# Keys and queries in one row, first weights in runs of 4 KB, another written list for block 0

## The chip, the core and the metric

The kernel runs on one core of a Trainium2 chip. The core has five engines with an instruction queue each: TensorE (PE in the rows; its weight loads are PEld), VectorE (DVE), ScalarE (ACT), GpSimd (POOL) and SyncE (SP), which here only starts DMA transfers. Each engine runs its own instructions strictly in the order in which they were written; engines wait for each other at semaphores. The metric is the device time of one execution in microseconds (us).

## What is computed

Sparse attention over 8 batches, 8 heads, 576 positions and head size 64, then a feed-forward layer of 4608 tokens with inner size 2048, in float32:

```python
scores = np.matmul(q, k.transpose(0, 1, 3, 2)) / np.sqrt(D)
mask_local = (rel >= 0) & (rel < 32)              # heads 0 to 3
mask_strided = (rel >= 0) & (col % 32 == row % 32) # heads 4 to 7
attn = softmax(where(mask, scores, -1e9))
x = (attn @ v).transpose(0, 2, 1, 3).reshape(B * S, H * D)   # 4608 x 512
h = x @ w_in                                       # 512 x 2048, kept as float64
out = (h / (1 + exp(-h))) @ w_out                  # 2048 x 512, kept as float64
```

## The kernel before

**Attention.** A batch is cut into six groups (`GROUPS`): three of local heads (12 tiles of 32 queries), three of strided heads (8, 8 and 6 tiles). Group number c counts on over the batches: 0 to 5 are batch 0, 6 to 13 belong to the next ones. A group needs its keys and queries (`load_qk`, line 384, into the tile `k`) and its values (`load_v`, into `v`).

**Feed-forward.** Tokens are taken in nine blocks of 512. Matrix products run with each operand split into a high and a low part, three matmuls for one product. The weights come as 64-bit numbers in 32 pieces of 512 KB (`load_piece`, line 343): piece 0 is columns 0 to 127 of `w_in`, after that `w_in` and `w_out` take turns. Block 0 is computed while the weights arrive; each piece is rounded and split on ACT and DVE, and stays in the core.

**The written list.** From the first instruction to the last product but one of block 0, the order of the work is a list of words, `PLAN` (line 145), that `Steps.follow` (line 204) carries out word by word. So the list fixes the order on every engine. The words, with c a group, n a piece and f a chunk of 128 inner columns (0 to 15):

- Attention: `kc` and `vc` loads; `Sc` scores on PE (line 485); `Mc` mask and row minimum on DVE (L513); `Ec` exp on ACT (L531, 6 or 8 steps); `Rc` reciprocal (DVE, L546 and L547); `Nc` scaling (L550); `Tc` transpose on PE and `Pc` its copy out (L560); `Vc` transpose on DVE (L578, L583, groups from 6 on); `Oc` times values (PE, L617, L622 or L637); `Qc`, `Xc` turn a local result back; `Bc` copy of the result into x (L649, L677, L693).
- Weights: `pn` load; `an` two ACT passes (L312, L317); `jn` join (DVE, L323); `bn` high part (L368); `dn` low part (DVE, L372).
- Block operands: `Hbc` and `Lbc`, high (L710) and low part (L714) of columns c of x for block b. `H00` to `L03` belong to block 0, `H10` to `L13` to block 1.
- Chunks of block 0: `hf` and `if`, the two halves of the inner product (PE, L722, 6 matmuls each); `tf` tanh (ACT, L732); `gf` gate (DVE, L754); `wf` and `lf`, high and low part of the gated chunk (L762, L766); `of` the output product (PE, L781, 12 matmuls). Chunk f uses piece 2f-1 of `w_in` (piece 0 for f = 0) and piece 2f+2 of `w_out` (piece 31 for f = 15).
- `~m` is m filler matmuls of 128 columns (PE, L889). `.A`, `.D`, `.P` choose ACT, DVE or POOL where a step may run on several.

The list ends with `o14`. Behind it a planner with fixed costs orders the rest (blocks 1 to 8); the first work there is the inner product of chunk 0 of block 1 on PE, 12 matmuls (L722), then the last output product of block 0.

**Loads.** SP starts nearly all transfers. In batch 0 a group's keys and queries are two transfers (lines 390 and 392; the queries of the first three groups start from ACT); later one transfer of two runs per partition, both as long as the longer of the two (line 388). A piece of `w_in` comes as four runs of 1 KB per partition (line 355), a piece of `w_out` as one run of 4 KB (line 360); the first six pieces in two halves.

Of the kernel before, what the change touches and what calls it, by code (L numbers as in the profile page):

```python
# [107 lines left out]
class Group:  # L108
    def __init__(self, local, first, count):
        self.local, self.first, self.count = local, first, count  # L110
        self.rows = STRIDE if local else KW
# [8 lines left out]

        self.at = [(t % self.n, t // self.n) for t in range(count)]
# [25 lines left out]
M4 E4 Q0 k6 C1 v3 v4 T1 P1.D R2 S3 M3 E3 X0 B0.D a1 T2 P2.D O1 p0 C2 Q1 R4 N4.P S5 M5 k7 O2 X1  # L147
Q2 B1.A R3 N3.D ~2 j1 T4 P4.A E5 H00.D p3 p4 k8 X2 B2.A T3 P3.D a0 L00.P H01.A O4 p5 p2 O3 S6
b1.D B4 R5 N5.D d1 j0 b0.A L01.P T5 P5.D d0 p6 B3 H02.D L02 ~4 O5 B5 H03.D L03 a3 M6 j3
b3.D E6 h0 h1 p7 R6 v7 d3 i0 t0 g0 S8 M8 k10 a5 j5 i1 S7 M7 a2 j2 p9 b5.A d5 w0.D t1 g1  # L150
b2.A d2 h2 p11
S10 l0 i2 a6 j6 v6 h3 a7 j7 o0 a4 i3 b6.D w1.D b7.A p8 j4 d7 t2 g2 h4 b4.A d4 l1 o1 k12 p13 a11
# [6 lines left out]
b21.A d21 b25.A d25 p27 t10 g10 t9 g9 h11 S11 k13 h12 i11 i12 Y0 E9 V7 M11 a24 j24 b24.D d24
p26 w10.A w9.A l9 o9 a27 j27 b27.A l10 t11 g11 t12 S12 g12 d27 M12 E11 R11 N11 a26 j26 O7 B7 v9  # L160
R9 N9 b26.A d26 o10 w11.A l11 w12.A l12 O10 V9 V11 B10 E12 R12 p29 a29 j29 p28 a28 j28 h13 h14
i13 t13 g13 i14 t14 g14 b28.A d28 N12 b29.A d29 O9 V12 v11 B9 o11 w13.A o12 w14.A l14 l13 O11
# [54 lines left out]
def sparse_attention_ffn(ctx: ExitStack, tc: tile.TileContext, kqt, vt, w_in, w_out, out):  # L217
# [165 lines left out]

    def load_qk(a):
        to, of = kbds[kbd_of(a.b, a.at)], kqt[a.b, a.gi]
        if a.b:
            n = max(a.g.nq, a.g.nk)
            load(out=to[:, :, :n], in_=of[:, :, :n])
            return
        load(out=to[:, 0, : a.g.nk], in_=of[:, 0, : a.g.nk])  # L390
        way = nc.scalar.dma_start if a.at < 3 else load
        way(out=to[:, 1, : a.g.nq], in_=of[:, 1, : a.g.nq])

    def load_v(a):
# [418 lines left out]
    def attention_steps(c, due, last=None):  # L813
# [6 lines left out]
        cols = 2 * max(a.g.nq, a.g.nk) if a.b else a.g.nq + a.g.nk  # L820
        k = add(f"k{c}", {"SP": P * cols * 4 / RATE}, t0 - 6, [], lambda: load_qk(a),
                writes=[k_place])
# [1630 lines left out]
```

## Time and profile before

| | us |
|---|---|
| Runs | 807.27, 812.03, 813.08 (median 812.03) |
| Span of the profiled execution | 808.0 |
| PE busy in it | 797.0 (99%) |
| DVE busy | 602.9 (75%) |
| ACT busy | 583.3 (72%) |
| POOL busy | 112.2 (14%) |
| Share of PE in the chain that ended last | 93% |

The profile shows one execution. Its views: the time line of an engine (start, length, engine, line, operation, result<-inputs, count, and in brackets the idle time before it with what ended it); the table of stretches (busy time of each engine and the granted TensorE clock); the transfers by line with their size and the time from start to landing. Successive instructions overlap a little, so the time that a row takes of its engine is best read as the distance to the next row's start.

### The profile page before, as it was taken

What the parts mean: (1) busy time and instruction counts of PE and PEld (TensorE: products, weight loads), DVE (VectorE), ACT (ScalarE), POOL (GpSimd) and SP (SyncE); (2) the same over time, 40 slices, a digit from 0 to 9 for tenths busy, and PEclk for the clock granted to TensorE, in tenths of its full rate; (3) what the DMA queues carried; (4) which work ended last, traced back from release to release, by engine and by line L of the source; (5) the groups of instructions that cost most, each with busy time, mean ns of one, the idle gap of its engine ahead of it and who ended that gap; (6) DMA issues with size and microseconds to landing.
All of it is one profiled execution on the core that took longest, in us unless ns stands there. A gap on an engine that the chain in (4) does not pass through costs nothing.

```text
span 808.0 us, 18904 instructions
## 1 busy us (share of the span) xinstructions
PE 797.0 (99%) x6661; PEld 659.7 (82%) x6661; DVE 602.9 (75%) x1660; ACT 583.3 (72%) x1559; POOL 112.2 (14%) x160
## 2 busy tenths in 40 slices
PE   8999999999999999999999999999999999999998
PEld 5688778888888898888888888888888888888887
DVE  6999896757868898955789999644699945557753
ACT  7999886557688988898895997788846534445451
POOL 6300004667000000015203000000230000000000
PEclk9999999999999999999999999999999999999999
DMA  8987455588999868698887976896567696666676
GB/s 265 316 258 233 133 189 167 208 271 281 310 288 333 263 220 276 225 319 288 296 269 218 277 249 195 242 280 193 181 195 216 197 269 194 194 194 194 194 215 155
DMA packets 150909, 191.13 MB, mean 237 GB/s; under 512 B 38240, under 2 KB 91104, under 8 KB 150816
## 3 DMA queue, kind: packets, MB, share of 16 engines
q1 hardware_dynamic: 149296, 189.21, 74.8%
q8 instruction: 53, 0.87, 0.4%
q10 hardware_dynamic: 1520, 0.72, 0.3%
q14 instruction: 40, 0.33, 0.1%
HBM read 151.09 MB, written 38.80 MB: 235 GB/s over the span
## 4 chain that ended last, share of the span: by engine, by line
PE 93%; DMA 3%; DVE 2%; ACT 1%; issue 1%; SPq 0%; POOL 0%; POOLq 0%; DVEq 0%
PE ps L1586 33%; PE po L2188 19%; PE po L781 16%; PE ps L722 10%; PE ps L2188 6%; PE ps L637 2%; DMA k<-kqt 2%; PE ps L485 1%; PE po L2331 1%; PE po L637 1%; PE ps L476 1%; PE ps L889 1%; DMA v<-vt 1%; DVE stage L2168 1%; ACT stage L2164 0%
## 5 line engine op out<-in xcount | busy, mean ns | idle before, releaser
L1586 PE MATMUL ps<-xop,w 128*128 128x512 f32 (+1 forms) x720 | 143.7, 348 | 0.0
L1586 PE MATMUL ps<-w,w 128*128 128x512 f32 x576 | 138.6, 390 | 0.0
L1586 PEld LDWEIGHTS ps<-xop,w 128*128 128x128 f32 x720 | 118.2, 189 | 18.5
L1586 PEld LDWEIGHTS ps<-w,w 128*128 128x128 f32 x576 | 107.9, 188 | 22.5
L531 ACT ACTIVATE sm<-sm,sums 128x54 f32<-128x54 f32 (+2 forms) x320 | 109.4, 345 | 7.8 <-DVE sums L513 7.7
L2188 PE MATMUL po<-stage,w 128*128 128x512 f32 x456 | 107.0, 390 | 0.0
L2188 PEld LDWEIGHTS po<-stage,w 128*128 128x128 f32 x456 | 85.3, 188 | 17.8
L722 PE MATMUL ps<-xop,w 128*128 128x512 f32 x384 | 94.9, 394 | 0.0
L722 PEld LDWEIGHTS ps<-xop,w 128*128 128x128 f32 x384 | 71.0, 188 | 15.2
L531 ACT ACTIVATION_READ_ACCUMULATOR sm<-sm,sums 128x1 f32 x320 | 60.6, 189 | 0.0
L781 PE MATMUL po<-w,ghi 128*128 128x512 f32 x168 | 52.1, 391 | 0.0
L2168 DVE TENSOR_TENSOR stage<-w,stage 128x512 fp32r<-128x512 f32 x56 | 40.9, 733 | 13.0 <-ACT stage L2164 12.5
L2164 ACT CAST stage<-w 128x512 fp32r<-128x512 f32 x56 | 34.8, 621 | 20.0 <-DVE stage L2168 8.1
L2026 DVE TENSOR_TENSOR w<-ps,w 128x512 f32<-128x512 f32 x44 | 30.0, 686 | 25.2 <-PE ps L1586 24.6
L2064 ACT ACTIVATE w<-w 128x512 f32<-128x512 f32 x45 | 27.6, 629 | 18.6 <-DVE w L2026 18.4
L766 DVE TENSOR_TENSOR glo<-th,ghi 128x512 fp32r<-128x512 f32 x48 | 34.7, 727 | 7.1 <-ACT ghi L762 6.9
L2188 PE MATMUL ps<-stage,w 128*128 128x512 f32 x168 | 39.4, 391 | 0.0
L503 POOL MEMSET sm<- 128x80 f32 (+1 forms) x18 | 2.9, 161 | 247.9 <-ACT pt L604 74.8
L2188 PEld LDWEIGHTS ps<-stage,w 128*128 128x128 f32 x168 | 31.4, 188 | 6.6
L2022 ACT COPY w<-ps 128x512 f32<-128x512 f32 x48 | 27.9, 584 | 12.0 <-PE ps L1586 10.7
L732 ACT ACTIVATE th<-ps 128x512 f32<-128x512 f32 x32 | 18.8, 592 | 24.5 <-PE ps L722 23.5
L604 ACT COPY pt<-sm 32x192 f32<-32x192 f32 (+1 forms) x96 | 34.8, 362 | 1.8
(330 smaller groups left out, 1639.7 us busy)
## 6 DMA issues: line engine op xcount, KB each, us to landing
w<-sums SPq DMA_DIRECT2D x208, 256.0 KB, 3.2
w<-osums SPq DMA_DIRECT2D x160, 256.0 KB, 2.9
sums<-xop SPq DMA_DIRECT2D x16, 512.0 KB, 3.8
osums<-stage SPq DMA_DIRECT2D x16, 512.0 KB, 5.5
v<-vt SPq DMA_DIRECT2D x21, 384.0 KB, 5.2
stage<-w_out SPq DMA_DIRECT2D x14, 512.0 KB, 4.3
k<-kqt SPq DMA_DIRECT2D x14, 477.0 KB, 5.6
stage<-w_in SPq DMA_DIRECT2D x12, 512.0 KB, 4.1
```

The lines of the kernel that those rows point to most:

```text
L531: nc.scalar.activation(out=self.s_sb[:, c, h], in_=self.s_sb[:, c, h], func=AF.Exp, bias=self.peaks[:, c, h : h + 1], scale=-1.0, accum_ou ...
L604: copy[by](out=self.pt[to, odd], in_=of)
L722: nc.tensor.matmul(ph, weight(0, wi, fc)[:, cc // 2, cc % 2 * P : (cc % 2 + 1) * P], x[xi][cc], start=(cc, n) == (0, 0), stop=(cc, n) == ( ...
L766: either[engine].tensor_sub(out=g[1][:, cols], in0=th[:, cols], in1=g[0][:, cols].bitcast(F32))
L781: nc.tensor.matmul(po[tt], g[gi][:, cols], weight(1, wi, fc), start=first and n == 0, stop=last and n == 2,)
L1586: nc.tensor.matmul(bank[:, : right.shape[-1]], left(wi, kt), right[:, kt, xi], start=first and (kt, n) == (0, 0), stop=(kt, n) == (1, 2), ...
L2022: copy_ps(out=unit(place), in_=of())
L2026: nc.vector.tensor_add(out=to, in0=of(), in1=to)
L2064: nc.scalar.activation(out=unit(out), in_=source(), func=AF.Silu)
L2164: copy_ps(out=gated_ops(to.slot)[0], in_=unit(place))
L2168: nc.vector.tensor_sub(out=lo, in0=unit(place), in1=hi.bitcast(F32))
L2188: nc.tensor.matmul(bank(name, key, m), left[:, wi, m * P : (m + 1) * P], right[xi], start=first and (j, i) == (0, 0), stop=(j, i) == (FH - ...
```

## The change

Three things are changed. The arithmetic stays.

1. Keys and queries of a group lie behind each other in one row per partition. In batch 0 they come in two transfers that are the two halves of the row; later in one transfer of one run. The padding to the longer of the two goes: 477 KB become 459.5 KB, 448 become 416, 416 become 400, 359 become 346.5.
2. `w_in` is laid out on the host so that a piece is one run of 4 KB per partition, as `w_out` was.
3. `PLAN` is another list of the same steps. Some steps change engine (B1, H01, b0, b4, b5, b12, b13, b29, w13, H11 to DVE; P5, H03, b6, b8, b23, b24, b30, b31, w1 to ACT). The fillers grow from 24 units to 44.

```diff
@@ load_piece
-        if layer == 0:
-            to = stage.rearrange("p (c f) t -> p c (f t)", c=NP)
-            of = w_in[:, cols].bitcast(I32).rearrange("(c p) f -> p c f", p=P)
-            for some in halved(NP, 2 if i < AHEAD else 1):
-                load(out=to[:, some], in_=of[:, some])
-        else: ...
+        to = stage.rearrange("p f t -> p (f t)")
+        of = (w_out if layer else w_in)[cols, :].bitcast(I32)
+        for some in halved(2 * DM, 2 if i < AHEAD else 1):
+            load(out=to[:, some], in_=of[:, some])
@@ load_qk
-        if a.b:
-            n = max(a.g.nq, a.g.nk)
-            load(out=to[:, :, :n], in_=of[:, :, :n])
-            return
-        load(out=to[:, 0, : a.g.nk], in_=of[:, 0, : a.g.nk])
-        way = nc.scalar.dma_start if a.at < 3 else load
-        way(out=to[:, 1, : a.g.nq], in_=of[:, 1, : a.g.nq])
+        for some in halved(a.g.cols, 1 if a.b else 2):
+            way = nc.scalar.dma_start if some.start and a.at < 3 and not a.b else load
+            way(out=to[:, some], in_=of[:, some])
@@ PLAN, its first line and its last two
-k0 k1 k2 v0 ~7 S0 v1 M0 k4 E0 k3 v2 C0 ~1 S1 k5 M1 E1 ~3 S2 M2 p1 E2 v5 T0 P0.D R1 ~7 S4 O0 R0
-B11 H10.A L10 H11.A h15 S13 M13 L11 p30 a30 j30 b30.D d30 i15 t15 g15 p31 a31 j31 b31.D d31
-H12.A H13.A L12 L13 o13 w15.A l15 o14 E13 R13 N13 V13
+k0 ~7 S0 k1 v0 ~5 S1 M0 M1 k2 E0 E1 ~8 T0 S2 R0 C0 v1 k4 v2 P0.D M2 C1 O0 k3 k5 R1 T1 Q0 E2 P1.D
+H11.D o12 l13.D R13 N13.D h15 H12.A g14 w14.A j30 H13.A b30.A l14.D L13.D o13 d30.D a31 j31 i15
+t15 b31.A g15 w15.A d31.D l15.D E12 V13 L11.D R12 o14 L12.D N12.D V12 L10.D
```

The new list moves work at three places that matter below. The first is ACT in the first quarter of block 0. Before, behind the exps of groups 0, 1, 2, 4 and 3 (34 steps together) stand a1, B1, P4, then E5 (6 steps), B2, a0:

```order
L531 ACTIVATE sm,sums<-sm,sums 128x64 x34
L312 ACTIVATE stage_303<-stage_303 128x512
L317 ACTIVATE stage_303<-stage_303 128x512
L693 COPY xb<-po 128x3x4x32
L560 COPY pt<-po 128x512
L531 ACTIVATE sm,sums<-sm,sums 128x64 x6
L693 COPY xb<-po 128x3x4x32
L312 ACTIVATE stage_485<-stage_485 128x512
L317 ACTIVATE stage_485<-stage_485 128x512
L710 CAST xop<-xb 128x512
L677 COPY xb<-po 128x8x18
L677 COPY xb<-po 128x15x18
```

After, E5 joins the first exps (40 steps), then P4, a0, B2, a1, P5 (line numbers are lower by 7 or 8, but for L312 and L317, which are L315 and L320):

```order
L524 ACTIVATE sm,sums<-sm,sums 128x64 x40
L553 COPY pt<-po 128x512
L315 ACTIVATE stage_492<-stage_492 128x512
L320 ACTIVATE stage_492<-stage_492 128x512
L686 COPY xb<-po 128x3x4x32
L315 ACTIVATE stage_499<-stage_499 128x512
L320 ACTIVATE stage_499<-stage_499 128x512
L553 COPY pt<-po 128x384
L670 COPY xb<-po 128x8x18
L670 COPY xb<-po 128x15x18
L670 COPY xb<-po 128x24x18
L670 COPY xb<-po 128x17x18
```

So E5 has moved ahead of a1 and P4, B1 has left ACT and P5 has come to it; B4 and B3 follow directly.

The second is the end of the list on DVE. Before, it ends with L12, L13 (two rows each), l15, R13, N13 and V13; the row behind is the gate of block 1:

```order
L714 TENSOR_TENSOR xop<-xb,xop 128x64
L714 TENSOR_TENSOR xop<-xb,xop 128x448
L714 TENSOR_TENSOR xop<-xb,xop 128x64
L714 TENSOR_TENSOR xop<-xb,xop 128x448
L766 TENSOR_TENSOR glo<-th,ghi 128x512
L546 TENSOR_SCALAR sums<-sums 128x8
L547 RECIPROCAL sums<-sums 128x8
L550 TENSOR_TENSOR sm<-sm,sums 128x8x54
L578 STREAM_TRANSPOSE pt<-sm 128x256 x2
L583 STREAM_TRANSPOSE pt<-sm 32x256 x4
```

After, V13 (its four small transposes are the first row here), L11, R12, L12, N12, V12 and, as the very last step, L10:

```order
L576 STREAM_TRANSPOSE pt<-sm 32x256 x4
L707 TENSOR_TENSOR xop<-xb,xop 128x64
L707 TENSOR_TENSOR xop<-xb,xop 128x448
L539 TENSOR_SCALAR sums<-sums 128x6
L540 RECIPROCAL sums<-sums 128x6
L707 TENSOR_TENSOR xop<-xb,xop 128x64
L707 TENSOR_TENSOR xop<-xb,xop 128x448
L543 TENSOR_TENSOR sm<-sm,sums 128x576
L571 STREAM_TRANSPOSE pt<-sm 128x192 x2
L576 STREAM_TRANSPOSE pt<-sm 32x192 x4
L707 TENSOR_TENSOR xop<-xb,xop 128x64
L707 TENSOR_TENSOR xop<-xb,xop 128x448
```

So L10, the low part of the first columns of x for block 1, has moved from before M13 to the end of all listed DVE work. On PE the second matmul behind o14, the (high weight, low x) product of chunk 0 of block 1, waits for it.

The third is PE around S13 (`ps<-k`, 16 rows in one). Before, i15 follows it and then o13:

```order
L722 MATMUL ps<-xop,w_8_667 128x512
L485 MATMUL ps<-k_82 64x54 x16
L722 MATMUL ps<-xop,w_8_665 128x512 x2
L722 MATMUL ps<-xop,w_8_667 128x512
L722 MATMUL ps<-xop,w_8_665 128x512 x2
L722 MATMUL ps<-xop,w_8_667 128x512
L781 MATMUL po<-stage_1654,ghi 128x512
```

After, S13 follows i14, and o12, h15, o13, i15 and o14 are still to come:

```order
L715 MATMUL ps<-xop,w_8_693 128x512
L478 MATMUL ps<-k_82 64x54 x16
L774 MATMUL po<-stage_1643,ghi 128x512
L774 MATMUL po<-stage_1646,ghi 128x512
L774 MATMUL po<-stage_1643,glo 128x512
```

So S13 has moved ahead by one output product (o12) and one half (h15). M13 on DVE, which S13 releases, is still the step from which the DVE tail above starts: behind M13 come g13, w13, H11, l13, R13, N13, g14, j30, l14, L13, d30, j31, g15, d31, l15 and then the rows shown.

## Rows read from the trace of the kernel before

**Rows 1.** Table of stretches: stretch, its length, busy us of each engine (instructions), granted clock.
```profile
36.00:60.00 24.00, 23.78 (x193) 19.56 (x194) 23.69 (x61) 23.80 (x62) 0.00 (x0) 1.00 0.81 254
```

**Rows 2.** Time line of PE: start, length, engine, line, result<-inputs, count, idle before.
```profile
24.65 0.91 PE L622 MATMUL po<-pt,v 64*64 64x54 f32 x24 [0.25 <-ACT xb L677]
25.49 4.38 PE L722 MATMUL ps<-xop,w 128*128 128x512 f32 x18
...
36.22 0.82 PE L485 MATMUL ps<-k 64*32 64x64 f32 x48 [1.21 <-DMA k<-kqt]
...
39.87 0.62 PE L781 MATMUL po<-w,ghi 128*128 128x512 f32 x2
```

**Rows 3.** Time line of ACT, the part before PE begins the feed-forward.
```profile
17.31 0.66 ACT L312 ACTIVATE stage<-stage 128x512 f32<-128x512 f32 x1
...
18.43 0.45 ACT L693 COPY xb<-po 128x384 f32<-128x384 f32 x1
...
19.46 0.35 ACT L531 ACTIVATE sm<-sm,sums 128x64 f32<-128x64 f32 x1
...
23.06 0.60 ACT L710 CAST xop<-xb 128x512 fp32r<-128x512 f32 x1
```

**Rows 4.** Time line of DVE in the same part, up to the first x operands.
```profile
17.75 0.62 DVE L661 TENSOR_TENSOR xq<-po,sums 128x192 f32<-128x192 f32 x2
...
20.87 1.11 DVE L368 CAST w<-stage 128x512 fp32r<-128x512 f32 x1
...
24.94 0.83 DVE L372 TENSOR_TENSOR w<-stage,w 128x512 fp32r<-128x512 f32 x1 [0.39 <-ACT w L368]
25.78 0.43 DVE L710 CAST xop<-xb 128x512 fp32r<-128x512 f32 x1
```

**Rows 5.** Transfers of the first 60 us: count, size, median us from start to landing.
```profile
stage<-w_out SPq DMA_DIRECT2D x6, 512.0 KB, 5.1
stage<-w_in SPq DMA_DIRECT2D x6, 512.0 KB, 4.9
```

**Rows 6.** Time line of PE from S13 to block 1's first product.
```profile
115.64 0.69 PE L485 MATMUL ps<-k 64*64 64x54 f32 x32
...
117.75 0.62 PE L781 MATMUL po<-stage,ghi 128*128 128x512 f32 x2
...
123.21 2.88 PE L722 MATMUL ps<-xop,w 128*128 128x512 f32 x12
```

**Rows 7.** Time line of DVE from 112 us on: V11, then M13 to V13.
```profile
112.45 0.63 DVE L578 STREAM_TRANSPOSE pt<-sm 128x192 f32<-128x192 f32 x2
113.11 1.52 DVE L583 STREAM_TRANSPOSE pt<-sm 32x192 f32<-32x192 f32 x4
...
116.55 0.21 DVE L513 CUSTOM_DVE_ANT_0 sm<-ps,mask_strided 128x54 f32<-128x54 f32 x1
...
117.61 0.76 DVE L714 TENSOR_TENSOR xop<-xb,xop 128x64 fp32r<-128x64 f32 x2
...
119.01 0.43 DVE L368 CAST stage<-stage 128x512 fp32r<-128x512 f32 x1
...
123.81 0.69 DVE L766 TENSOR_TENSOR glo<-th,ghi 128x512 fp32r<-128x512 f32 x1
...
124.85 0.61 DVE L550 TENSOR_TENSOR sm<-sm,sums 128x432 f32<-128x432 f32 x1
...
128.11 0.69 DVE L754 SCALAR_TENSOR_TENSOR th<-th,ps 128x512 f32<-128x512 f32 x1
```

**Rows 8.** Time line of PE: the first two fillers of seven units.
```profile
1.36 3.36 PE L889 MATMUL ps<-ident 128*128 128x512 f32 x4 [1.36 <-POOL ident masks.py:199]
...
8.86 1.67 PE L889 MATMUL ps<-ident 128*128 128x512 f32 x4
```

**Rows 9.** Table of stretches, columns as in rows 1: the end of the program.
```profile
804.00:806.00 2.00, 0.32 (x3) 0.12 (x1) 0.45 (x1) 0.00 (x0) 0.00 (x0) 1.00 0.57 95
...
807.30:808.00 0.70, 0.00 (x0) 0.00 (x0) 0.00 (x0) 0.00 (x0) 0.00 (x0) 0.50 0.00 0
```

More of the change, by code (lines that the diff above doesn't have):

```diff
@@ L119, in __init__ @@
         self.nk = self.k0[-1] + KW
+        self.kq = [("k", 0, self.nk), ("q", 0, self.nq)]
+        self.cols = self.nk + self.nq
+        self.q0 = [self.nk + q for q in self.q0]
         self.at = [(t % self.n, t // self.n) for t in range(count)]
@@ L145 @@
 PLAN = """
-k0 k1 k2 v0 ~7 S0 v1 M0 k4 E0 k3 v2 C0 ~1 S1 k5 M1 E1 ~3 S2 M2 p1 E2 v5 T0 P0.D R1 ~7 S4 O0 R0
[L147 to L152, printed above, removed]
@@ L159 @@
[L159 to L162, printed above, removed]
-B11 H10.A L10 H11.A h15 S13 M13 L11 p30 a30 j30 b30.D d30 i15 t15 g15 p31 a31 j31 b31.D d31
-H12.A H13.A L12 L13 o13 w15.A l15 o14 E13 R13 N13 V13
+k0 ~7 S0 k1 v0 ~5 S1 M0 M1 k2 E0 E1 ~8 T0 S2 R0 C0 v1 k4 v2 P0.D M2 C1 O0 k3 k5 R1 T1 Q0 E2 P1.D
@@ new lines @@
+S4 X0 M4 E4 R2 B0.D O1 C2 S3 T2 Q1 ~4 X1 M3 S5 k6 v4 p0 P2.D R4 p1 M5 ~6 O2 E3 v3 N4.P v5 p3 ~6
+T4 S6 B1.D R3 Q2 N3.D M6 E5 P4.A R5 ~3 T3 a0 X2 P3.D H00.D O4 N5.D B2.A p5 ~5 T5 k7 j0 L00.P a1
+P5.A H01.D B4 O3 p4 B3 b0.D j1 d0.D b1.D L01.P O5 B5 h0 H02.D p2 d1.D L02.D H03.A L03.D p7 a3 a5
+j3 h1 b3.D p6 j5 i0 E6 b5.D i1 d3.D t0 d5.D p9 t1 h2 g0 g1 S7 a4 R6 a2 h3 i2 a7 w0.D i3 j4 l0.D
+j2 b2.A j7 d2.D a6 b7.A b4.D t3 o0 d4.D d7.D p11 w1.A g3 l1.D h4 a9 j6 j9 M7 a11 o1 k8 b9.A S8
+d9.D b6.A p10 w3.A t2 a10 p8 k10 d6.D p13 j11 p15 b11.A g2 p12 i4 N6.D v6 j10 w2.A h5 d11.D l2.D
@@ new lines @@
+w10.A d18.D j25 d24.D l10.D S11 i11 p26 b25.A t11 E9 h12 d25.D b20.A M11 o8 w9.A p27 h13 g11 S12
+a26 V7 d20.D M12 i13 i12 a27 l9.D j26 O7 R9 b26.A j27 d26.D B7 b27.A v9 p28 t12 o9 k13 E11 O10
+N9.D w11.A B10 o10 d27.D V9 l11.D p29 R11 O9 v11 o11 a28 B9 g12 w12.A a29 N11.D V11 j28 b28.A
+h14 j29 d28.D O11 l12.D b29.D i14 d29.D B11 S13 M13 t13 t14 H10.A p30 E13 g13 p31 w13.D a30
+H11.D o12 l13.D R13 N13.D h15 H12.A g14 w14.A j30 H13.A b30.A l14.D L13.D o13 d30.D a31 j31 i15
+t15 b31.A g15 w15.A d31.D l15.D E12 V13 L11.D R12 o14 L12.D N12.D V12 L10.D
@@ L241, in sparse_attention_ffn @@
     vbds = [vbd[:, i] for vbd in vbds for i in range(2)]
-    kbds = [const.tile([P, 2, QW], F32, name=f"k{i}") for i in range(KFIRST)]
+    kbds = [const.tile([P, 2 * QW], F32, name=f"k{i}") for i in range(KFIRST)]
     ident = const.tile([P, P], F32, name="ident")
@@ L486, in scores @@
                         self.pss[h][rows, c * self.seen : (c + 1) * self.seen],
-                        kbd[at, 1, g.q0[t] : g.q0[t] + g.rows],
-                        kbd[at, 0, g.k0[t] : g.k0[t] + self.seen], start=True, stop=True,
+                        kbd[at, g.q0[t] : g.q0[t] + g.rows],
+                        kbd[at, g.k0[t] : g.k0[t] + self.seen], start=True, stop=True,
                     )
@@ L819, in attention_steps @@
         k_place, v_place = f"k{kbd_of(a.b, a.at)}", f"v{vbd_of(a.b, a.at)}"
[L820 to L821 removed]
+        k = add(f"k{c}", {"SP": P * a.g.cols * 4 / RATE}, t0 - 6, [], lambda: load_qk(a),
                 writes=[k_place])
@@ L1945, in gated_ops @@
         if OWN_GOPS not in gated_halves and i >= OWN_GOPS:
-            ks = [const.tile([P, 2, T], F32R, name=f"k{n}") for n in range(2)]
-            more = [k[:, half] for k in ks for half in range(2)]
+            ks = [const.tile([P, 2 * T], F32R, name=f"k{n}") for n in range(2)]
+            more = [k[:, half * T : (half + 1) * T] for k in ks for half in range(2)]
             v = const.tile([P, VT * D * 2], F32R, name="v0")
@@ L2385 @@
     none = NP * S
-    q_from = np.full((NG, QW), none)
+    q_from = np.full((NG, 2 * QW), none)
     k_from = np.full((NG, QW), none)
@@ L2431 @@
     turned = np.arange(DM).reshape(4, 4, 32).transpose(1, 0, 2).reshape(-1)
-    kq = np.ascontiguousarray(np.stack([columns(k, k_from), columns(q, q_from)], axis=3))
+    kq = np.zeros((B, NG, P, 2 * QW), q.dtype)
+    of = {"k": columns(k, k_from), "q": columns(q, q_from)}
+    for gi, g in enumerate(GROUPS):
+        at = 0
+        for name, first, n in g.kq:
+            start = first + (g.nk if name == "q" else 0)
+            kq[:, gi, :, at : at + n] = of[name][:, gi, :, start : start + n]
+            at += n
+    w_in = moe_w_in.reshape(NP, P, NFC, P)
     arrays = {
@@ L2437 @@
         "vt": rows(v, v_from),
-        "w_in": np.ascontiguousarray(moe_w_in).view(np.int64),
+        "w_in": np.ascontiguousarray(w_in.transpose(2, 1, 0, 3)).reshape(DFF, DM).view(np.int64),
         "w_out": np.ascontiguousarray(moe_w_out[:, turned]).view(np.int64),
```

21 lines of the change are left out of this document (8 added, 13 removed).

## The prediction

> **What bounds the kernel now.** I read the table of stretches first, then the time lines of PE, ACT and DVE in block 0, then the transfers. From 36 us on PE is busy almost without a gap, but in block 0 it isn't alone: in the stretch from 36 to 60 us PE has 23.78 of 24.00 us, DVE 23.69 and ACT 23.80 [rows 1]. So an earlier product on PE is worth what it saves only where DVE and ACT have its operands ready. Before 36 us PE waits for others. The first half product, h0, starts at 25.49, right behind O5; the scores of group 7 still wait 1.21 us for keys; and the first output product, o0, starts at 39.87 [rows 2]. At the other end of the list all fits: M13 follows S13, and PE starts block 1's first product at 123.21 without a wait [rows 6], while DVE works on its list until 128.11 [rows 7]. The change touches these two ends: what the front gains, the tail can take back.
>
> **The loads.** A piece of `w_in` in runs of 1 KB lands 4.9 us after its start, a piece of `w_out` of the same size in runs of 4 KB after 5.1 us [rows 5]. So longer runs buy no landing time that shows, and I cost them at 0. Keys and queries shrink by 4 to 7 per cent (477 to 459.5 KB). The one load of keys that PE waits for in the front is that of group 7, 1.21 us [rows 2]; in the new order S7 comes later than its keys by the queue's order, so this wait goes with the front's gain below and isn't counted twice. Bounds for all loads together: no loss, at most 0.5 us of gain further on. I take 0.
>
> **The front: PE's lead.** On ACT, before, a1, B1, P4, E5, B2 and a0 take 17.31 to 23.06, 5.75 us; E5 starts at 19.46 in the midst of them [rows 3]. After, E5 follows the earlier exps, so it starts 2.15 us earlier, at 17.31. Up to P5, for which O5 waits, ACT has P4, a0, B2 and a1 (the 5.75 without B1's 0.55) and P5, a copy of about 0.5 (B1, of the same size, has 0.45): 17.31 + 5.20 + 0.5 = 23.0. O5 takes 0.84 (24.65 to 25.49) [rows 2], so h0 can start at 23.9, 1.6 us earlier.
>
> DVE comes too late for all of that. Before, from Q2 at 17.75 to the end of d0 at 25.78 it has 8.03 us, with 0.39 of waiting in it [rows 4]. In the new list the same stretch lacks b1 (1.03, 20.87 to 21.90, slow beside POOL's work), d1 (0.6) and P5 (0.5), and holds M6 (0.8, six of the eight steps of M13's 1.06 [rows 7]) and the casts B1, H01 and b0 (0.47, 0.33 and 0.33, estimates between 0.33 and the 0.46 of the cast at 119.01 [rows 7]): 8.03 - 0.39 - 2.13 + 1.93 = 7.44, so d0 ends at 25.2, or at 25.9 where b0 has b1's trouble with POOL. The third matmul of h0 waits for it. From there I add 0.6 for each of DVE's full-width steps and 0.35 to 0.46 for a cast: L03 ends 2.6 us later, d3 2.5 us after that, g1 1.8 us after that, d2 3.7 us after that, at 35.8 to 36.5. PE meanwhile does h0, h1, i0, i1, h2, S7, h3, i2 and i3, each half product 1.36 (12 matmuls take 2.73, 24 of them 117.75 to 123.21 [rows 6]), and waits for d0, for d1 and, before the second half of S7, for g0, some 1.5 us together. o0 then starts at 36.5 to 37.2 instead of 39.87, with the same work done (i3 in place of S8 and S10). The lead is 2.7 to 3.4; I take 3.0. The bounds: 0, if ACT and DVE lose it again before 110 us; 4.5, if DVE is never late.
>
> **The tail: what L10 costs.** Before, S13 starts at 115.64, M13 0.91 later at 116.55, and PE reaches the second matmul of block 1 at 123.21 + 0.23 = 123.44 [rows 6, 7]. After, S13 stands one output product and one half earlier, 1.5 x 2.73 = 4.09 us, and all is earlier by the lead of 3.0: S13 starts at 108.55, M13 at 109.46. Behind M13 DVE has the listed steps up to L10, and PE's second matmul of block 1 waits for L10. What these steps take: before, M13 to the end of V13 is 116.55 to 128.11, 11.56 us. The new stretch has all of it but two casts b (0.46 each, 119.01 to 119.47), and besides g13, g14 and l14 (0.6 each, a little under the 0.69 of l15's row, since rows overlap), l13 and R12 (1.04 together, as l15 and R13 from 123.81 to 124.85), w13 (0.46), H11 (0.5, two casts), N12 (0.6), V12 (2.2, as V11 from 112.45 to the end of its last row) and L10 (0.67, 117.61 to 118.28) [rows 7]. That is 11.56 - 0.92 + 7.27 = 17.9 us. L10 ends at 109.46 + 17.9 = 127.4, PE's matmul follows at 127.5: **4.0 us later** than before. In general the loss is 7.0 minus the lead. On PE stand only S13 and four times 2.73 behind S13's start, so PE is through with o14 at about 120.2 and then idle for some 7 us. This is the new stall: work of DVE (V13, V12, L11, L12) that nobody waits for at once now stands in front of the step for which PE waits.
>
> **The clock.** The first fillers of seven units took 3.36 us, the same seven units at 8.86 took 1.67 [rows 8]: PE starts on the lower of its two levels, 1.2 GHz, and reaches 2.4 GHz. At the end of the program PE's last work is done at 804.3, the granted clock is 1.00 until 806 and 0.50 from 807.3 on [rows 9]. So an idle time of 7 us can drop the clock, and the restart of block 1 then loses what the program's start loses, 3.36 - 1.67 = **1.7 us**. Bounds: 0 (the clock stays) and 3.4 (twice as long on the lower level). The Trainium skill, TensorE: Matmul & The Clock Gate, Part 1, says that an idle TensorE is throttled to half its clock and gets it back only after sustained activity. The end of this trace agrees for the fall, its start for the return; in the midst of the program no idle time is long enough to show it.
>
> **Sum.** 4.0 + 1.7 + 0 = 5.7 us slower. Behind the list the order of the instructions is the same as before, and PE has hardly a wait that such a shift could fill. On the profiled execution's 808.0 that is 813.7. The three runs and this execution (807.27, 812.03, 813.08, 808.0) have a mean of 810.1, 1.9 below the runs' median of 812.03; I put the sum on this mean: **815.8**.
>
> **Rivals.**
> - *PE doesn't wait for L10, the lead stays.* It decides at 11 us: if DVE's steps from M13 to L10 took no more than PE's work from S13 to o14 (0.6 + 4 x 2.73 = 11.5, less the 0.91 to M13), the kernel would be 3.0 us faster, 807.1. Against it: 17.9 from rows, and the order on DVE is strict.
> - *The lead is lost* (DVE as late as before at every step, or pieces landing late, since p0 and p1 come sooner behind the keys): 7.0 + 1.7 = 8.7 slower, 818.8. For it: DVE, ACT and PE are all near full from 36 to 60 us [rows 1]; against it: the sums of the front.
> - *The clock stays at 2.4 GHz*, or drops late: 4.0 slower, 814.1.
> - *The loads do what the words say and more*: keys that land earlier in later blocks and a front that gains 4.5 leave 810 to 811, no change.
>
> **How the numbers follow.** Forecast (lead 2 to 4, lower clock at the restart) 0.58; lead lost 0.16; clock stays 0.14; no change 0.07; lead kept 0.05. Forecast alone: 814 to 818. The range reaches down to 809, past the 811 of no change but without the lead kept, and up to 822, the lost lead with twice the clock's loss. One per cent (8.1 us) is about what a measurement here can tell from no change: slower by more needs the lost lead with the clock's full loss or runs that scatter upwards, 0.13; faster by more is out of reach of all cases but for scatter, 0.02; within it 0.85.
>
> **What would show it.** In the profile after: h0 near 24 to 25 us and o0 near 37; S13 near 108.5, M13 right behind; DVE without a gap from M13 to L10 for about 18 us; on PE a wait of about 7 us before block 1's first product, ended by DVE L707; the granted clock 0.50 for some us behind it. The prediction is wrong if that wait is under 3 us, if o0 is not earlier than 39, or if PE's later blocks show new waits.

## The result, and the profile after

| | before | after |
|---|---|---|
| Median of the runs (us) | 811.0 (4 runs) | 820.83 (4 runs: 820.41 to 823.85) |
| Ratio, 95% interval | 1 | 1.0144 (1.0109 to 1.0179) |
| Span of the profiled execution | 808.0 | 818.6 |
| o0 starts | 39.87 | 40.81 |
| S13 starts | 115.64 | 113.38 |
| PE's second matmul of block 1 | 123.44 | 133.16 |

By the ratio the changed kernel is 1.44 per cent slower, 11.7 us. The quotient of the two medians would be 1.0121: the four runs before scatter from 807.27 to 813.08, and in the later comparisons, with 17 to 29 runs of it, the kernel before has medians of 809.01 to 809.25. In the changed kernel's profile PE waits once for long, where the prediction said, but the lead that the front was to bring is not there.

The end of the list, PE's time line of the changed kernel (columns as in [rows 2]; it answers to [rows 6]):

```profile
113.38 0.69 PE L478 MATMUL ps<-k 64*64 64x54 f32 x32
...
125.03 0.39 PE L715 MATMUL ps<-xop,w 128*128 128x512 f32 x1
133.16 5.06 PE L715 MATMUL ps<-xop,w 128*128 128x512 f32 x11 [7.74 <-DVE xop L707]
138.02 0.69 PE L774 MATMUL po<-stage,ghi 128*128 128x512 f32 x2
```

Behind S13 PE has work for 11.65 us, then block 1's first matmul, and then 7.74 us of nothing until L10 is done. DVE in the same stretch (answers to [rows 7]):

```profile
114.12 0.21 DVE L506 CUSTOM_DVE_ANT_0 sm<-ps,mask_strided 128x54 f32<-128x54 f32 x1 [1.48 <-PE ps L478]
...
122.02 0.69 DVE L326 SCALAR_TENSOR_TENSOR stage<-stage 128x512 int32<-128x512 int32 x1 [0.35 <-ACT stage L320]
123.14 0.69 DVE L747 SCALAR_TENSOR_TENSOR th<-th,ps 128x512 f32<-128x512 f32 x1 [0.43 <-ACT th L725]
...
125.92 1.79 DVE L576 STREAM_TRANSPOSE pt<-sm 32x256 f32<-32x256 f32 x4
127.74 0.76 DVE L707 TENSOR_TENSOR xop<-xb,xop 128x64 fp32r<-128x64 f32 x2
...
132.34 0.76 DVE L707 TENSOR_TENSOR xop<-xb,xop 128x64 fp32r<-128x64 f32 x2
```

M13 waits for S13, and from its start at 114.12 to the end of L10 (132.34 + 0.76 = 133.10) DVE needs 18.98 us, 0.78 of it waits for ACT. The table of stretches around the wait (columns as in [rows 1]) has the clock:

```profile
126.00:130.00 4.00, 0.00 (x0) 0.00 (x0) 3.90 (x11) 0.65 (x4) 0.00 (x0) 0.74 0.00 0
130.00:133.00 3.00, 0.00 (x0) 0.00 (x0) 2.88 (x9) 0.00 (x0) 0.00 (x0) 0.50 0.00 0
133.00:138.00 5.00, 4.84 (x11) 3.80 (x12) 0.10 (x1) 0.00 (x0) 0.00 (x0) 0.50 0.00 0
```

With PE idle the granted clock falls from 1.00 to 0.50 (from 2.4 GHz to the lower level, 1.2 GHz), and the eleven matmuls behind the wait take 138.02 - 133.16 = 4.86 us, 0.44 each in place of 0.227.

The front, PE's time line of the changed kernel (answers to [rows 2]; L881 are fillers, L549 the transposes T4 and T5, L478 x48 the scores S6):

```profile
18.74 1.56 PE L881 MATMUL ps<-ident 128*128 128x512 f32 x4
20.14 0.60 PE L549 MATMUL po<-ident,sm 128*128 128x128 f32 x4
20.67 0.72 PE L478 MATMUL ps<-k 64*32 64x64 f32 x48
...
24.00 1.35 PE L881 MATMUL ps<-ident 128*128 128x512 f32 x4
25.18 0.49 PE L549 MATMUL po<-ident,sm 128*128 128x128 f32 x3
...
27.37 0.73 PE L715 MATMUL ps<-xop,w 128*128 128x512 f32 x2
28.96 6.95 PE L715 MATMUL ps<-xop,w 128*128 128x512 f32 x28 [0.85 <-DVE w L369]
...
40.81 0.61 PE L774 MATMUL po<-w,ghi 128*128 128x512 f32 x2
```

h0 starts at 27.37, not at 25.49 as before nor at the predicted 23.9, and its third matmul waits for d0. DVE there (answers to [rows 4]; L326 are the joins j0 and j1):

```profile
21.52 0.23 DVE L506 CUSTOM_DVE_ANT_0 sm<-ps,mask 128x64 f32<-128x64 f32 x1 [1.31 <-PE ps L478]
...
23.65 0.55 DVE L543 TENSOR_TENSOR sm<-sm,sums 128x384 f32<-128x384 f32 x1
24.12 1.76 DVE L326 SCALAR_TENSOR_TENSOR stage<-stage 128x512 int32<-128x512 int32 x1
...
26.47 1.76 DVE L326 SCALAR_TENSOR_TENSOR stage<-stage 128x512 int32<-128x512 int32 x1
28.16 0.74 DVE L369 TENSOR_TENSOR w<-stage,w 128x512 fp32r<-128x512 f32 x1
```

And POOL, with N4 and the low parts L00 and L01:

```profile
17.39 1.05 POOL L543 TENSOR_TENSOR sm<-sm,sums 128x512 f32<-128x512 f32 x1 [3.76 <-ACT sm L524]
23.81 1.52 POOL L707 TENSOR_TENSOR xop<-xb,xop 128x512 fp32r<-128x512 f32 x1 [5.37 <-DVE xop L703]
26.30 1.39 POOL L707 TENSOR_TENSOR xop<-xb,xop 128x512 fp32r<-128x512 f32 x1 [0.96 <-DVE xop L703]
```

Two things are to be seen. T4 needs N4, which ends at 18.44; PE is in six units of fillers until 20.14. The scores behind T4 come late, and M6 on DVE waits 1.31 us for them. T5 is held up in the same way: N5 ends at 24.20, T5 starts at 25.18. Second, each join takes 1.76 us where it took 0.69 (the row below, kernel before), beside an operation of POOL, and ends 0.55 us behind that operation's end (25.88 and 25.33; 28.23 and 27.69).

```profile
19.33 0.69 DVE L323 SCALAR_TENSOR_TENSOR stage<-stage 128x512 int32<-128x512 int32 x1
```

Two suspects, then, for the lost lead: the fillers and POOL. The tail and the clock have one each, L10 and the idle time.

Not all of the loss lies ahead of o0. From o0 to S13 PE is busy all the time in both kernels and takes 75.77 us before and 72.57 after, 3.20 less and not the 4.09 that the prediction counts for S13's new place. So 0.9 us of the lead goes there without a wait, and it does so in every run with the new list (72.56 or 72.57 in each). The record doesn't show why.

### The profile page after: what moved, and what is told of

Its sections match the earlier page's. It is cut to its first block, busy times and chain, and to the rows that moved or that the text cites. A ratio compares the mean times of both kernels' runs of the same rounds, so it can differ in the third digit from the quotient of the medians.

```text
span 818.6 us, 18929 instructions
## 1 busy us (share of the span) xinstructions
PE 803.7 (98%) x6673; PEld 663.1 (81%) x6673; DVE 604.3 (74%) x1662; ACT 583.4 (71%) x1557; POOL 114.1 (14%) x160
## 4 chain that ended last, share of the span: by engine, by line
PE 92%; DVE 4%; ACT 3%; SPq 1%; issue 0%; DMA 0%; POOL 0%; POOLq 0%; ACTq 0%
PE ps L1578 33%; PE po L2180 19%; PE po L774 16%; PE ps L715 11%; PE ps L2180 5%; PE ps L630 2%; PE ps L478 1%; PE po L2323 1%; PE po L630 1%; PE ps L469 1%; PE ps L881 1%; ACT sm L524 1%; ACT pt L597 1%; DVE stage L2160 1%; SPq L396 1%
## 5 line engine op out<-in xcount | busy, mean ns | idle before, releaser
L1578 PEld LDWEIGHTS ps<-w,w 128*128 128x128 f32 x576 | 107.9, 188 | 22.5
L715 PE MATMUL ps<-xop,w 128*128 128x512 f32 x384 | 97.4, 402 | 8.6 <-DVE xop L707 7.7
L2018 DVE TENSOR_TENSOR w<-ps,w 128x512 f32<-128x512 f32 x44 | 30.0, 685 | 25.2 <-PE ps L1578 24.6
L725 ACT ACTIVATE th<-ps 128x512 f32<-128x512 f32 x32 | 19.2, 601 | 37.2 <-PE ps L715 34.5
L747 DVE SCALAR_TENSOR_TENSOR th<-th,ps 128x512 f32<-128x512 f32 x32 | 21.8, 683 | 26.0 <-ACT th L725 25.9
## 6 DMA issues: line engine op xcount, KB each, us to landing
k<-kqt SPq DMA_DIRECT2D x14, 459.5 KB, 5.0
```

The source lines that it names most:

```text
L715: nc.tensor.matmul(ph, weight(0, wi, fc)[:, cc // 2, cc % 2 * P : (cc % 2 + 1) * P], x[xi][cc], start=(cc, n) == (0, 0), stop=(cc, n) == ( ...
L1578: nc.tensor.matmul(bank[:, : right.shape[-1]], left(wi, kt), right[:, kt, xi], start=first and (kt, n) == (0, 0), stop=(kt, n) == (1, 2), ...
L2018: nc.vector.tensor_add(out=to, in0=of(), in1=to)
```

## The experiments

Each time stands against the kernel before, run in the same comparison on the same chip, and the ratio is that of the comparison. The runs e1 to e4, e5 to e7 and e8 to e10 are three comparisons on three chips. A difference between two runs is that of their medians; by the ratios it comes out up to half a microsecond larger or smaller.

### Loads or list: e2_loads and e3_list

The change has parts that can be taken one by one: e2_loads is the changed kernel with the list of before, e3_list the kernel before with the new list.

```diff
@@ e2_loads, against the changed kernel
-k0 ~7 S0 k1 v0 ~5 S1 M0 M1 k2 E0 E1 ~8 T0 S2 R0 C0 v1 k4 v2 P0.D M2 C1 O0 k3 k5 R1 T1 Q0 E2 P1.D
+k0 k1 k2 v0 ~7 S0 v1 M0 k4 E0 k3 v2 C0 ~1 S1 k5 M1 E1 ~3 S2 M2 p1 E2 v5 T0 P0.D R1 ~7 S4 O0 R0
...
@@ e3_list, against the kernel before: the same lines the other way round
```

> Parts 1 and 2 of the change alone: keys and queries in one row and w_in in runs of 4 KB, with the list of the kernel before. Theory (the loads are hidden): within 0.2 per cent of the kernel before, 809.5 to 812.5 us, o0 again near 39.9 us. Rival (the loads help the later blocks, where the changed kernel lost some 3 us less in its stalls from 230 to 280 us): 807 to 809 us. Rival (pieces or keys come later and cost the front): 813 us or more, and o0 behind 40.5 us.

Measured: 807.99 us, ratio 0.9985 (0.9971 to 0.9998).

> Part 3 alone: the new list with the transfers of the kernel before. Theory (the list makes the whole difference): 819.5 to 822.5 us, with h0 near 27.4, o0 near 40.8 and the wait for L10 of 7 to 8 us. Rival (the new loads cost the front 1 to 3 us): 817 to 819 us, with o0 at 38 to 40 us.

Measured: 821.30 us, ratio 1.0144 (1.0127 to 1.0162), the ratio of the whole change.

So the list is the whole loss. The loads alone gain 0.15 per cent, 1.2 us, with an interval that just clears 1; the prediction took 0 with at most 0.5. In the trace of e2_loads S7 no longer waits for its keys (before 1.21 us [rows 2]), and o0 starts at 39.26, 0.6 earlier. The gain is within the 0.2 per cent of the theory, but its rival, that the loads help the later blocks, is true as well: at the last product e2_loads is 1.5 us ahead (801.21 against 802.73). The kernel before waits there 0.16 and 0.22 us for transfers near 240 us, and 0.71 us near 257 us without a named releaser; e2_loads has none of the three. The landing times speak for no difference by the length of the runs: w_in pieces of 512 KB land after 5.1 us in e3_list, with runs of 1 KB, and after 4.3 in e2_loads and 5.4 in the changed kernel, with runs of 4 KB.

### The tail: e1_tail

```diff
-H11.D ... l14.D L13.D o13 d30.D ... V13 L11.D R12 o14 L12.D N12.D V12 L10.D
+H11.D ... l14.D L13.D L10.D L11.D L12.D o13 d30.D ... V13 R12 o14 N12.D V12
```

> The changed kernel, with the three steps L10, L11, L12 moved from the end of the list to the place behind L13 (some 5 us of DVE work ahead of V13); nothing else. Theory (the new stall is only the place of L10): PE's wait of 7.7 us at 125 us goes, the granted clock stays at 1.00 (2.4 GHz) there, so the 2.2 us of slow matmuls behind the wait go too; DVE still ends its list at 133.1, so the gate of block 1's first chunk comes some 5 us later than in the kernel before, and PE may wait up to 2 us for it at its output product near 133 us: 808.5 to 811.5 us, 0 to 0.5 per cent from the kernel before. Rival (DVE as a whole is behind, the wait only changes its place): the wait stands again at the output product of block 1's first chunk with 5 us or more, and the time is 815 us or more.

Measured: 813.52 us, ratio 1.0051 (1.0033 to 1.0069), 7.3 us less than the changed kernel. PE's time line of e1_tail:

```profile
17.73 0.46 PE L478 MATMUL ps<-k 64*64 64x64 f32 x14 [1.32 <-issue]
...
125.25 0.50 PE L774 MATMUL po<-stage,ghi 128*128 128x512 f32 x1 [1.03 <-DVE stage L369]
...
127.87 2.88 PE L715 MATMUL ps<-xop,w 128*128 128x512 f32 x12
```

The first row is a hold-up of S5 in the front that the changed kernel's execution doesn't have (see the last section). The wait for L10 is gone, and block 1's first product runs at full speed, 12 matmuls in 2.72 us (127.87 to 130.59). A smaller wait has come, 1.03 us for d30, because the three steps now stand ahead of it; the theory looked for one at the output product of block 1 instead. The time lies 2 us above the range of the theory and 1.5 below that of the rival. So the place of L10 made the large wait, and what is left, 4.5 us to the kernel before, is this small wait and the front.

### The front: e5_fill, e6_port, e7_both

All three stand on e1_tail, so that the front is seen alone.

```diff
@@ e5_fill, and in e7_both
-... E1 ~8 T0 ... Q1 ~4 X1 ... M5 ~6 O2 ... p3 ~6 T4 ... R5 ~3 T3 ... p5 ~5 T5 ...
+... E1 ~5 T0 ... Q1 ~1 X1 ... M5 ~1 O2 ... p3 T4 ... R5 T3 ... p5 T5 ...
@@ e6_port, and in e7_both
-... j0 L00.P a1 ... b1.D L01.P O5 ...
+... j0 L00.D a1 ... b1.D L01.D O5 ...
```

> The kernel of e1_tail with fewer fillers in the front: the six fillers of 8, 4, 6, 6, 3 and 5 units ahead of T0, X1, O2, T4, T3 and T5 become 5, 1, 1, 0, 0 and 0, so 23 units are left in place of 44 (before: 24). 21 units are 4.5 us of PE at 2.4 GHz (0.215 a unit by the 32 units of e4_clock). In the trace of the changed kernel T4 starts 1.4 us behind the end of N4, T5 1.0 us behind the end of N5, and M6 on DVE waits 1.31 us for the scores that stand behind T4's fillers. Theory 1 (the fillers held PE longer than the waits that they covered, and that alone lost the front): 3.5 to 4.5 us less than e1_tail, 809 to 810 us, h0 at 23.5 to 24.5. Theory 2 (DVE's joins, held up by POOL, set the start as well): d0 still ends near 27.4, PE waits for it, and only 1.3 to 2 us come back: 811.5 to 812.3 us. Rival 3 (the front is set by ACT and DVE, the fillers lie in their shadow): no change, 813 us or more.

The edit as made takes out 25 units and leaves 19, not 21 and 23, here and in the runs built on it; at 0.215 a unit that is 5.4 us of PE.

Measured: 809.96 us, ratio 1.0010 (0.9998 to 1.0021). 3.6 us less than e1_tail, as theory 1 has it. h0 starts at 25.50, 3.4 earlier than in e1_tail (28.89), but a microsecond later than theory 1 said, and h0's third matmul still waits 1.44 us for d0 (PE's time line of e5_fill), as theory 2 has it:

```profile
25.50 0.74 PE L715 MATMUL ps<-xop,w 128*128 128x512 f32 x2
27.68 6.94 PE L715 MATMUL ps<-xop,w 128*128 128x512 f32 x28 [1.44 <-DVE w L369]
```

> The kernel of e1_tail with L00 and L01 (the low parts of the first two column blocks of x) on DVE instead of POOL; fillers as in the changed kernel. In its trace the joins j0 and j1 on DVE take 1.76 us beside POOL's L00 and L01, otherwise 0.69. Theory 2 (POOL's operation holds DVE up): j0 and j1 take 0.7 us, DVE saves 2.1 and pays 1.3 for the two steps; d0 ends some 1.5 us earlier, PE's wait of 0.85 us behind h0's second matmul goes: 0.8 us less than e1_tail, 812.4 to 813 us. Rival (a join of that place is slow for another reason): j0 and j1 stay at 1.7 us, DVE ends later by 1.3, and the time is that of e1_tail or up to 1 us more, 813.5 to 814.5 us.

Measured: 811.11 us, ratio 1.0025 (1.0013 to 1.0036), 2.4 us less than e1_tail, more than the 0.8 expected, though the intervals of the two ratios touch. The joins on DVE (time line of e6_port):

```profile
25.08 0.68 DVE L326 SCALAR_TENSOR_TENSOR stage<-stage 128x512 int32<-128x512 int32 x1
25.68 0.68 DVE L707 TENSOR_TENSOR xop<-xb,xop 128x512 fp32r<-128x512 f32 x1
...
26.96 0.68 DVE L326 SCALAR_TENSOR_TENSOR stage<-stage 128x512 int32<-128x512 int32 x1
```

With POOL quiet a join takes 0.68: the 1.07 us on top were POOL's. Join and L00 together now take less (1.2) than the join alone did beside POOL. How much of the 2.4 this is, the traces bound: from h0 to o0 PE takes 13.44 us in e1_tail and 12.13 in e6_port, 1.3 less, with the wait of 0.85 for d0 gone. The rest can't be put down to POOL with any certainty, since e1_tail's execution has S5's hold-up of 1.32 us and e6_port's has none. The edit also changes more than the joins: POOL's building of further masks (L256, 8 in a row) stood behind L01 at 29.4 us and now runs at 19.1, and DVE's later joins, 0.75 and 0.76 beside them in e1_tail, take 0.69.

> Both edits, e5_fill's 23 units and e6_port's L00 and L01 on DVE, on top of e1_tail. If the fillers and POOL's hold on DVE are the two reasons for the lost lead, they add up to more than each alone: h0 starts near 24, its third matmul without a long wait, o0 near 37.5 to 38.5, and 3 to 4.5 us less than e1_tail: 809 to 810.5 us. If one of them is enough, the time is that of the better of e5_fill and e6_port within 0.5 us. If DVE and ACT lose the lead again before the tail (both are near full from 36 to 60 us), o0 is early but S13 is not, and the time stays above 811.5 us.

Measured: 809.29 us, ratio 1.0000 (0.9990 to 1.0010), 4.2 us less than e1_tail and 0.7 less than e5_fill, whose interval overlaps; in the traces S13 is 0.98 earlier than in e5_fill. The two gains, 3.6 and 2.4, don't add up. A reading that fits the rows: h0's third matmul starts with the later of PE (held by the fillers) and DVE (held by POOL), and what one edit frees the other still holds. h0 starts at 25.89 and o0 at 38.60, which is 2.2 earlier than in the changed kernel, but not the 36.5 to 37.2 of the prediction. The fronts beside each other (starts in us, one execution each):

| | h0 | o0 | S13 | S5 held up |
|---|---|---|---|---|
| before | 25.49 | 39.87 | 115.64 | 0.78 |
| changed kernel | 27.37 | 40.81 | 113.38 | 0 |
| e1_tail | 28.89 | 42.33 | 114.90 | 1.32 |
| e5_fill | 25.50 | 39.58 | 112.15 | 1.15 |
| e6_port | 28.34 | 40.47 | 113.04 | 0 |
| e7_both | 25.89 | 38.60 | 111.17 | 0 |

### The lead and the wait: e9_front

e7_both's front with the changed kernel's tail.

```diff
@@ against e7_both: the end of the list as in the changed kernel
-... l14.D L13.D L10.D L11.D L12.D o13 d30.D ... E12 V13 R12 o14 N12.D V12
+... l14.D L13.D o13 d30.D ... E12 V13 L11.D R12 o14 L12.D N12.D V12 L10.D
```

> The changed kernel with e7_both's front and its own tail (L10 the last step on DVE). Theory (what S13 gains is passed on one to one, since M13 and all of DVE's tail follow S13; the wait for L10 stays at 7.5 to 8 us and the clock falls as before): the front's 4.1 us come off the changed kernel: 816 to 817.5 us. Rival (DVE's tail is tied to something that doesn't move with S13, its weights or ACT): the wait for L10 grows by what PE gains, and the time is 819 us or more.

Measured: 817.89 us, ratio 1.0102 (1.0084 to 1.0120), 2.9 less than the changed kernel (3.4 by the ratios) where the theory looked for 4.1, and 0.4 above the theory's range. PE's time line:

```profile
110.72 0.69 PE L478 MATMUL ps<-k 64*64 64x54 f32 x32
...
122.37 0.39 PE L715 MATMUL ps<-xop,w 128*128 128x512 f32 x1
130.49 5.06 PE L715 MATMUL ps<-xop,w 128*128 128x512 f32 x11 [7.74 <-DVE xop L707]
```

S13 is 2.66 us earlier than in the changed kernel, PE's second matmul 2.67, and the wait is 7.74 in both. So a lead is handed on one to one, and it doesn't shorten the wait: DVE's steps from M13 to L10 follow S13 too.

### The clock: e4_clock and e10_fclock

```diff
-... V12 L10.D
+... V12 L10.D ~32
```

> The changed kernel with 32 units of fillers as the last word of the list, so that PE works on them (32 x 0.239 = 7.6 us at 2.4 GHz) in the time in which it waited for L10; what it waits for is not changed. Theory (the clock fell because PE had nothing to do): the granted clock stays at 1.00, block 1's first product runs at 0.23 us a matmul instead of 0.43, and the time is 2.2 us less: 818.1 to 819.1 us. Rival (the clock fell for another reason, or the fillers delay block 1 by as much as they save): 820 us or more.

Measured: 820.07 us, ratio 1.0129 (1.0110 to 1.0147), only 0.8 less than the changed kernel, in the rival's range. Between the two profiled executions the fronts differ: in e4_clock S5 is held up by 1.36 us and the fillers of 5 units at 5.5 us take 2.31 instead of 1.35. The two medians, of four and five runs from different comparisons, don't settle it either. So the edit was made again on e9_front, both in one comparison.

> e9_front with 32 units of fillers as the last word of the list, in PE's wait for L10 (6.5 us of it by the rows of e4_clock). Only the clock behind the wait is changed, with the front the same in both. Theory (PE's idle time lowers the clock): block 1's first product at 0.23 us a matmul, granted clock 1.00, and 2.0 to 2.4 us less than e9_front. Rival (the fillers hand back what they save): less than 1 us.

Measured: 816.21 us, ratio 1.0084 (1.0066 to 1.0101), 1.7 less than e9_front; the two intervals overlap, so the size is rough. PE's time line of e10_fclock:

```profile
123.45 7.03 PE L881 MATMUL ps<-ident 128*128 128x512 f32 x16
129.92 0.80 PE L715 MATMUL ps<-xop,w 128*128 128x512 f32 x1
131.58 2.79 PE L715 MATMUL ps<-xop,w 128*128 128x512 f32 x11 [0.87 <-DVE xop L707]
```

and its table of stretches:

```profile
126.00:133.00 7.00, 6.13 (x18) 3.10 (x17) 5.34 (x16) 0.00 (x0) 0.00 (x0) 1.00 0.00 0
133.00:138.00 5.00, 5.00 (x24) 4.14 (x23) 1.38 (x2) 2.78 (x6) 0.00 (x0) 1.00 0.04 15
```

The work that PE waits for is as late as ever: the second matmul starts 19.78 us behind S13 (111.80), in e9_front 19.77. But with fillers in the wait the granted clock stays at 1.00, and the eleven matmuls behind it take 2.63 us to the next row (134.21) instead of 4.86, 2.2 less. It was the idle time that lowered the clock. The two fronts are not the same in these executions: in e10_fclock S5 is held up by 1.70 us (e9_front 0.98), the granted clock is 0.50 from 20 to 23 us, and S13 is 1.08 later.

### A better tail: e8_best

```diff
-... L13.D L10.D L11.D L12.D o13 d30.D ... d31.D l15.D ...
+... L13.D o13 d30.D L10.D ... d31.D L11.D L12.D l15.D ...
```

> e7_both's front (23 units of fillers, L00 and L01 on DVE) with a better tail: only L10 stands behind d30, L11 and L12 stand behind d31, in place of all three ahead of d30. In e7_both PE waits 1.2 us for d30 at the first matmuls of o14 because L10 to L12 (2.0 us) stand ahead of it. Theory: this wait goes and none takes its place (L10 ends near 120.1, PE needs it at 123.2): 1.0 to 1.2 us less than e7_both, 807.9 to 808.4 us, level with or just under the kernel before. Rival (the wait moves to L11 or L12 in block 1's first product, or to its first output product): 809 us or more.

Measured: 808.72 us, ratio 0.9987 (0.9974 to 1.0000). Block 1 starts at 121.97, 1.24 before the kernel before [rows 6], with no wait for d30 or L10. But at the output product of block 1's first chunk a wait of 0.88 us appears, put down to ACT (time line of PE in e8_best):

```profile
121.97 2.88 PE L715 MATMUL ps<-xop,w 128*128 128x512 f32 x12
127.41 2.88 PE L715 MATMUL ps<-xop,w 128*128 128x512 f32 x12
131.18 0.73 PE L774 MATMUL po<-k,ghi 128*128 128x512 f32 x2 [0.88 <-ACT stage L787]
```

ACT comes to L787, which copies finished results out of `po`, only behind the gated chunk's high part, which at 130.01 had waited 4.45 us for DVE's gate, and the gate stands behind the end of DVE's list. So the new list's longer DVE tail still costs something when L10 is out of it. The time is 0.6 less than e7_both, where the theory looked for 1.0 to 1.2. e8_best and e2_loads are level, 0.13 and 0.15 per cent under the kernel before; e8_best's interval reaches 1.

## Why the prediction was right or wrong, point by point

- **What bounds the kernel, and where to look** (right). The change acted at the two ends named. The sums for the loads, 0, missed a gain of 1.2 us.
- **The tail** (right). The loss was put at 7.0 us minus the lead, with 17.9 us on DVE from M13 to L10 and a wait of some 7 us. Measured were 18.98 and 7.74. With the lead as it was (below), 7.0 + 1.8 = 8.8 us of delay come out; PE's second matmul is 133.16 - 123.44 = 9.7 late. The 0.9 missing are DVE's two waits for ACT (0.78) and 0.3 in the sizes of its steps, less 0.2 because M13 follows S13 sooner (0.74 in place of 0.91).
- **The clock** (right in kind, a little small). 1.7 us was forecast for the restart. The eleven matmuls took 4.86 us, at 0.227 they would take 2.5: 2.4 us in the trace, 1.7 between the medians of e9_front and e10_fclock. The start of the program, from which the price was taken, is a weaker witness than it seemed: the first fillers do take twice as long [rows 8], but the granted clock reads 1.00 there, from 0 to 9 us.
- **The front** (wrong; this is the step that failed). S13 was to come at 108.55, with a lead of 3.0; it came at 113.38, which against 115.64 - 4.09 = 111.55 is a lead of -1.8, outside the bounds of 0 and 4.5; o0 at 40.81 is also the prediction's own sign of being wrong (not earlier than 39). Of the -1.8, 0.9 lies ahead of o0 (40.81 against 39.87) and 0.9 between o0 and S13, where the shift was counted as 4.09 and is 3.20. The sum for ACT started E5 at 17.31 and let P5 follow at 22.5, and the sum for DVE ended d0 at 25.2 or 25.9; P5 came at 25.77, d0 ended at 28.83. The 3.6 us of d0 can all be named: 1.31 is M6's wait for the scores behind T4's fillers, 2.14 the two joins, 0.21 a wait for ACT. In the front three terms were missing or too small:
  - *The fillers.* They grew from 24 units to 44, the text of the change says so, and the prediction gave them no price. Between 5 and 28 us PE's fillers take 9.73 us in the changed kernel against 4.69 before. They were taken as filling waits; but a filler that is still running when the operand arrives is a wait of its own. e5_fill put a price on 25 of them: 3.6 us.
  - *POOL beside DVE.* The prediction had the pattern in hand, "b1 (1.03, 20.87 to 21.90, slow beside POOL's work)", and allowed 0.7 for it at b0. In the new order the joins stand beside L00 and L01, and each loses 1.07. e6_port: 2.4 us by the medians, 1.3 of it seen between h0 and o0. The Trainium skill, SBUF — State Buffer, section "SBUF: two separate sides", has the rule: DVE and GpSimd share a pair of ports, a lock that whoever starts first holds for the whole instruction; it concerns a DVE operation in one of its two-port modes, or one with two inputs in SBUF against a GpSimd operation that reads SBUF. The trace agrees: both joins (two inputs, both in `stage`) start 0.3 and 0.2 us behind POOL's operation and end 0.55 us behind its end.
  - *The exps ahead.* The 40 exps on ACT end at 20.67, not at 17.31 + 2.15 = 19.46: S2 starts at 9.59 (before: 7.80), behind 20 units of fillers, and ACT waits 0.52 us for its rows and 0.22 for those of the next group. The stretch ahead of the moved step was taken over from before, though the list had changed there too. This part is seen in the trace; no run isolates it. In e7_both, too, P4 stands at 21.04 behind the exps, P5 at 24.28, and d0 ends at 26.52; its S13 at 111.17 gives a lead of 0.4. What keeps it from 3.0, beside the 0.9 behind o0, stays open.
- **The rival "the lead is lost"** gave 8.7 us. Of the cases priced it is the one that came nearest, for reasons that the prediction had not priced, and the lead was not only lost but negative. It had 0.16.
- **The sum.** By its terms: lead 3.0 too good by 4.8, the tail short by 0.9, the clock by 0.7, so 5.7 + 6.4 = 12.1 us late at the end of block 1's first product (138.02 against 125.93 before: 12.1). The span grew by 10.6 only. The rest comes back later: at the 253.99 of the row below, 242.37 before, 11.6 are left, and at the last product 10.5. Of these 1.6 us, 0.4 are the waits for transfers near 240 us that the changed kernel does not meet, and 0.7 is a wait near 257 us without a named releaser; the rest isn't traced.

Changed kernel, PE:

```profile
253.99 0.69 PE L630 MATMUL ps<-pt,v 64*64 64x54 f32 x32 [0.62 <-ACT xb L642]
...
813.26 1.60 PE L2323 MATMUL po<-stage,w 128*128 128x256 f32 x12
```

Kernel before, PE:

```profile
242.37 0.69 PE L637 MATMUL ps<-pt,v 64*64 64x54 f32 x32 [0.61 <-ACT xb L649]
257.00 0.44 PE L485 MATMUL ps<-k 64*64 64x54 f32 x12 [0.71 <-issue]
...
802.73 1.60 PE L2331 MATMUL po<-stage,w 128*128 128x256 f32 x12
```

The wait of 0.71 before 257.00 has no counterpart in the changed kernel. One more slip is in the level on which the sum was put: 808.0 is the span of the profiled execution, taken there as a run time, while the changed kernel's profiled run of 820.41 us has a span of 818.6, 1.8 less.

So the time, 820.83, lies in the range of 809 to 822, but the statement that it stays within one per cent of the kernel before, to which 0.85 was given, was wrong: the lead was counted as a gain of 3.0 against the tail, and it was a loss of 1.8. That the range holds the time is partly luck: its upper end was made of a lead of 0 and twice the clock's loss, and what came was a negative lead, a longer tail and a clock loss of 2.4.

## What to carry to other kernels

Price every operation that a new order adds, fillers too: a filler is free only if it ends before the operand of the work behind it arrives, so compare its end with the end of the producer. When a step moves on DVE, look at what POOL runs at its new place, and redo the stretch ahead of a moved step instead of taking its start from the old trace. The step that another engine waits for first belongs ahead of work for which nobody waits yet; here three words in the list were worth 7.3 us.

## What the runs showed of the hardware

- A wait of 7.74 us in the midst of the program brought the granted clock to 0.50, and it stayed there for the 4.9 us behind it. Fillers in the wait kept it at 1.00, which in this place saved 1.7 us by the medians, 2.2 in the traces.
- A join on DVE beside POOL's tensor-tensor operation: 1.76 us; alone: 0.68. The other way round, POOL's eight mask selections (L256) take 4.62 us in the changed kernel, at 27.89, where DVE is busy without a wait, and 2.84 in e6_port, at 19.10, where DVE waits for 1.40 us of it.
- S5, in the front, is held up in its midst by 0 to 1.7 us in the executions with the new list, and the profile names no releaser ("issue"): 0 in the changed kernel, e3_list, e6_port and e7_both, 0.69 in e8_best, 0.98 in e9_front, 1.15 in e5_fill, 1.32 in e1_tail, 1.36 in e4_clock, 1.70 in e10_fclock. In e1_tail the transfers of its keys start before 11.2 us and take 3.5, so they had landed, and it went on at 17.73. In the six executions with the hold-up a transfer of an instruction queue (q8) falls between 14 and 18 us; in the changed kernel, e3_list and e6_port it falls between 12 and 14, but e7_both has it late and no hold-up. The cause stays open. There is one trace of each kernel, and kernels with the same list up to S5 (changed kernel, e1_tail, e4_clock) differ by up to 1.36, so the absolute times of two single traces can differ by over 1 us for a reason that is not the edit. That is why edits of the front were judged by medians first.
